# Linear attention on one core: stores cut into two halves of 64 partitions, and a longer TensorE warm-up

## The chip, the cores and the metric

The kernel runs on one core of a Trainium2 chip. Its engines work side by side: TensorE multiplies matrices (the profile lists its matmuls as PE and its weight loads as PEld), VectorE (DVE), ScalarE (ACT) and GpSimd (POOL) work on elements, and SyncE (SP) issues most of the transfers, which sixteen DMA engines carry out. Each engine runs its own instructions in order and waits for the others through semaphores. A transfer raises its semaphore by 16 when all of it has landed.

The metric is the time of one execution on the device, in microseconds (us).

## The reference

For each of 32 heads, with 2048 rows of 128 values in q, k and v (bfloat16):

```python
phi_q = jnp.where(q > 0, q + 1, jnp.exp(q)) + 1e-6
phi_k = jnp.where(k > 0, k + 1, jnp.exp(k)) + 1e-6
kv = jnp.einsum("bhsd,bhse->bhde", phi_k, v)
z = jnp.einsum("bhsd->bhd", phi_k)
num = jnp.einsum("bhqd,bhde->bhqe", phi_q, kv)
den = jnp.einsum("bhqd,bhd->bhq", phi_q, z)[..., None] + 1e-6
return num / den
```

So per head 1.5 MB is read, 0.5 MB is written, and between them stand two elementwise functions, a 128 x 128 product summed over all rows, a second product, and a division.

## The kernel before

**Tiling.** A head is laid out as 128 partitions with 16 rows each (`rows`, line 260): a partition holds 4,096 contiguous bytes of k, of q or of the output. One transfer moves a head of one tensor, 512 KB. Loads have six buffers for each tensor (`NBI`), stores ten (`NBO`), each with a semaphore of its own.

**One head.** ScalarE takes exp(k) (L328), VectorE caps it at 1 (L334), GpSimd makes the positive part of k (L330) and adds the two for five of the sixteen tiles (L339). TensorE sums phi_k^T v and z into `kvz_ps` (L355), and ScalarE and VectorE copy that to `kvs_sb` (L363, L365). TensorE transposes q through an identity into `x_ps` (L373), ScalarE takes its exp in two halves (L384), ScalarE and VectorE its positive part (L387, L390), VectorE caps (L393). TensorE multiplies with `kvs_sb` into five banks of `o_ps` (`num`, L411 and L417). VectorE adds the epsilon to the denominators (L456), takes reciprocals (L460) and divides into `o_sb` (L432, L438); in the last three heads ScalarE shares the division (L447). SP stores the head (L472).

**Order.** No engine's order follows from the loops. `Plan.add` is given an engine and a key, a number that counts in heads; each engine runs its operations by rising key (`Plan.order`, L54). `Plan.emit` works out which semaphores an operation must wait for from the tiles that it reads and writes, and leaves out a wait that an earlier one already covers. A writer of an output buffer waits for all stores that still read it. TensorE's middle part, twenty-four heads, is a hardware loop of four turns.

**Transfers.** All loads but the first v go through SP (L320), at about seven to eight heads ahead of their use by key. A store has the key `late = h + 1.0 + 0.18 * h`, so stores slip further behind the loads from head to head; after the last load the remaining stores follow. The last two heads go out in pieces of 6 and 10, and of 6, 6 and 4 tiles, so that the end of the kernel waits for a small one. When all is issued, SP waits for each store semaphore in turn (L152).

**Start.** While the first loads travel, TensorE runs nine matmuls of 128 x 512 on zeros (`warm`, L282 to L290, added at L296). They share one weight load; the second to ninth are emitted by the helper `mm_held` at L277.

Of the kernel before, what the change touches and what calls it, by code (L numbers as in the profile page):

```python
# [11 lines left out]
def _ap(base: bass.AP, elem_offset: int, dims):  # L12
    return bass.AP(base.tensor, base.offset + elem_offset, [list(base.ap[0])] + [list(d) for d in dims])
# [162 lines left out]
def bass_standalone__linear_attn_elu__prompt_kernel(  # L176
# [8 lines left out]
    NT = 16  # L185
# [3 lines left out]
    NBI = 6  # L189
    NBO = 10  # L190
# [20 lines left out]

    PIECES = {NH - 2: ((0, 6), (6, NT)), NH - 1: ((0, 6), (6, 12), (12, NT))}
    EXTRA = {NH - 2: 0, NH - 1: 1}
    LOOP, TURNS = 3, 4

    qf = q.rearrange("b h s d -> (b h) s d")
# [2 lines left out]
    of = out.rearrange("b h s d -> (b h) s d")  # L219

    with ExitStack() as es:
        def sb(name, shape, dt):
            return es.enter_context(nc.sbuf_tensor(name, shape, dt))
# [14 lines left out]
        o_sb = sb("o_sb", [P, NBO, NT, D], bf16)  # L238
# [11 lines left out]
        def dma_sem(name):  # L250
            return dsems[name]

        for n, c in (("k", NBI), ("q", NBI), ("v", NBI), ("o", NBO + 3), ("x", 1)):
            for i in range(c):
                dsems[(n, i)] = es.enter_context(nc.semaphore(f"s_{n}{i}"))

        block = es.enter_context(nc.Block())
        pl = Plan()

        def rows(x, h):  # L260
            return x[h].rearrange("(p j) d -> p (j d)", j=NT)
# [7 lines left out]
               reads=[("id0",)], writes=[("ident",)])  # L269
# [5 lines left out]
        def mm_held(pe, out, lhsT, rhs, start, stop):  # L275

            return pe.add_instruction(mybir.InstMatmult(  # L277
                name=nc.get_next_instruction_name(), engine=mybir.EngineType.PE, ldweights=False,
                ins=[pe.lower_ap(rhs), pe.lower_ap(lhsT)], outs=[pe.lower_ap(out)], start_tensor_calc=start,
                stop_tensor_calc=stop, tile_size=(P, P), tile_position=(0, 0), bass_skip_group_check=True))  # L280

        def warm(n):  # L282

            def f(pe):
                for w in range(n):
                    o = o_ps[:, (2 + w % 3) * 512:(3 + w % 3) * 512]
                    w_sb, zeros = warm_sb[:, :], _ap(warm_sb[:, :], 0, [[0, 4], [1, P]])
                    last = mm_held(pe, o, w_sb, zeros, True, True) if w else pe.matmul(o, lhsT=w_sb, rhs=zeros, start=True, stop=True)
                return last
            return f  # L290
# [2 lines left out]

        pl.add("act", -9, lambda a: a.activation(rden_sb[:, 0, 0:1], warm_sb[:, 0:1], ACT.Exp), reads=[("warm",)],
               writes=[("rden", 0, 0)])
        pl.add("pe", -9, warm(9), reads=[("warm",)], writes=[("banko", 2), ("banko", 3), ("banko", 4)])  # L296

# [6 lines left out]
        for h in range(NH):  # L306
# [3 lines left out]
            bi, b2, b3, bo = h % NBI, h % 2, h % 3, h % NBO  # L310

            def load(name, buf, src, key, h=h, bi=bi):
# [4 lines left out]
                if name == "v":  # L317
# [11 lines left out]
                   reads=[("k", bi)], writes=[("ek", b2)])  # L329
            pl.add("pool", h, lambda g, bi=bi, b3=b3: g.tensor_scalar(rk_sb[:, b3, :], k_sb[:, bi, :], BIG, 0.0,  # L330
                                                                      op0=ALU.min, op1=ALU.max),
                   reads=[("k", bi)] + ([("emq", 1)] if h == 2 else []), writes=[("rk", b3), ("rkx", b3), ("phik", b3)])
            pl.add("dve", at("emk", -3 + 0.95),
                   lambda d, b2=b2, b3=b3: d.tensor_scalar(emk_sb[:, b3, :], ek_sb[:, b2, :], 1.0, EPS, op0=ALU.min, op1=ALU.add),  # L334
                   reads=[("ek", b2)], writes=[("emk", b3)])

            def added(x, b3=b3):
# [3 lines left out]
                reads=[("emk", b3), ("rkx", b3)] + ([("emq", (h - 1) % 3)] if h else []), writes=[("phik", b3)])  # L341

            def kv(pe, tiles, srcs, h=h, bi=bi, b3=b3):
                for j in tiles:
# [16 lines left out]
                   reads=[("emk", b3), ("rk", b3), ("v", bi), ("ones",), ("vones",)], writes=[("bankkv",)])  # L361
            pl.add("pe", at("kv", -1.2), lambda pe, kv=kv: kv(pe, ADD, (rk_sb,)), reads=[("phik", b3), ("v", bi)], writes=[("bankkv",)])
            pl.add("act", at("kvs", -0.95), lambda a, b3=b3: a.activation(kvs_sb[:, b3, 1:], kvz_ps[:, 1:NC], ACT.Copy),  # L363
                   reads=[("bankkv",)], writes=[("kvs", b3)])
            pl.add("dve", at("zs", -1 + 0.905), lambda d, b3=b3: d.tensor_scalar(  # L365
                kvs_sb[:, b3, 0:1], kvz_ps[:, 0:1], kvz_ps[:, NC:NC + 1], None, op0=ALU.add),
                   reads=[("bankkv",)], writes=[("zs", b3)])
# [14 lines left out]
            for half in (0, 1):  # L382
                pl.add("act", h - 1.1 + 0.05 * half,
                       lambda a, b2=b2, c=cols(half): a.activation(eq_sb[:, b2, c], xT_ps[:, c], ACT.Exp),  # L384
                       reads=[("bankx", half)], writes=[("eq", b2, half)])
            pl.add("act", h - 1.0,
                   lambda a, b3=b3, c=cols(1): a.activation(rq_sb[:, b3, c], xT_ps[:, c], ACT.Relu),  # L387
                   reads=[("bankx", 1)], writes=[("rq", b3, 1)])
            pl.add("dve", at("rq", -2 + 0.948),
                   lambda d, b3=b3, c=cols(0): d.tensor_scalar(rq_sb[:, b3, c], xT_ps[:, c], 0.0, None, op0=ALU.max),  # L390
                   reads=[("bankx", 0)], writes=[("rq", b3, 0)])
            pl.add("dve", at("emq", -2 + 0.955),
                   lambda d, b2=b2, b3=b3: d.tensor_scalar(emq_sb[:, b3, :], eq_sb[:, b2, :], 1.0, EPS, op0=ALU.min, op1=ALU.add),  # L393
                   reads=[("eq", b2, 0), ("eq", b2, 1)], writes=[("emq", b3)])
# [4 lines left out]
            def nbank(b, h=h):  # L399
                return ("bankx", b) if h == NH - 1 and b < 2 else ("banko", b)  # L400
# [20 lines left out]
            for bank in range(NB):  # L421
                pl.add("pe", h + 0.7 + 0.001 * bank, num(bank), reads=phi,
                       writes=[nbank(bank)] + ([nbank(0)] if bank == 1 else []))
# [28 lines left out]
            for g, (b0, b1, place_d, runs) in enumerate(groups):  # L452
# [6 lines left out]
                    reads=banks, writes=[("den", b3, g)])  # L459
                pl.add("dve", key + 0.01, lambda d, b3=b3, b0=b0, b1=b1: d.reciprocal(  # L460
                    rden_sb[:, b3, 4 * b0:4 * b1], den_sb[:, b3, 4 * b0:4 * b1]),
                    reads=[("den", b3, g)], writes=[("rden", b3, g)])
                if g == 0:
                    pl.add("dve", h + 0.911, last_tile, reads=[nbank(0), nbank(1), ("rden", b3, 0)], writes=[("o", bo, NT - 1)])
                for n, (eng, t0, t1, *place_a) in enumerate(runs):
                    pl.add(eng, h + place_a[0] if eng == "act" else key + 0.012 + 0.004 * n,
                           div_act(t0, t1) if eng == "act" else div(t0, t1),
                           reads=[nbank(b) for b in range(t0 // 3, (t1 + 2) // 3)] + [("rden", b3, g)],
                           writes=[("o", bo, t) for t in range(t0, t1)])

            def store(t0, t1, key, slot, h=h, bo=bo):
                pl.add("sp", key, lambda sp: sp.dma_start(rows(of, h)[:, t0 * D:t1 * D],  # L472
                                                          o_sb[:, bo, t0:t1].rearrange("p j d -> p (j d)")),
                       reads=[("o", bo, t) for t in range(t0, t1)], dma=("o", slot))

            late = h + 1.0 + 0.18 * h
            for n, (t0, t1) in enumerate(PIECES.get(h, ((0, NT),))):
                store(t0, t1, late + 0.01 * n, bo if n == 0 else NBO + EXTRA[h] + n - 1)

# [29 lines left out]
```

## Time and profile before

| what | value |
|---|---|
| time, median of three runs | 170.68 us (170.63 to 170.9) |
| profiled execution: time, and span from first to last instruction | 170.68 us, 168.8 us |
| granted TensorE clock, mean over the span | 0.994 |
| busy: PE, PEld, DVE, ACT, POOL | 158.0, 151.7, 149.6, 157.3, 105.5 us |
| moved by DMA | 67.31 MB, 399 GB/s on average |
| in the hardware queue that SP feeds | 22688 packets, 98.5% of 16 engines' span |
| stores of a whole head | 30 of 512 KB, 13.8 us from issue to landing at the median |
| SP waiting at the end for stores to land | 3.3 us |

The span is counted from the first to the last instruction; what lies around it makes up the rest of an execution's time. Busy times of TensorE are modelled, since matmuls are pipelined. A DMA's time to landing counts from its issue, so it holds the time in the queue. "DMA share" is the mean busy share of the sixteen DMA engines, and can pass 1 by a little because records of packets overlap.

### The profile page before, as it was taken

To read this page: it belongs to the slowest core of one execution; us is meant where nothing else is said; L and a number is where in the kernel's file an instruction comes from. 1 tells how busy PE (TensorE), PEld (TensorE's weight loads), DVE (VectorE), ACT (ScalarE), POOL (GpSimd) and SP (SyncE) were. 2 spreads that over 40 slices of the span, in tenths; PEclk is the share of its full clock that TensorE was granted. 3 is DMA by queue.
4 is the path that set the end of the run, shared out by engine and by line. 5 is a ranking of instruction groups with operands and counts; after the bars stand their busy time and mean duration, and the time that the engine had idled before them with its cause. 6 is when DMAs were issued, how large, how long until landed. Compare 5 with 4: busy or idle time off the path is not lost.

```text
span 168.8 us, 6570 instructions
## 1 busy us (share of the span) xinstructions
PE 158.0 (94%) x3089; PEld 151.7 (90%) x2401; DVE 149.6 (89%) x293; ACT 157.3 (93%) x180; POOL 105.5 (62%) x72
## 2 busy tenths in 40 slices
PE   7588999999999999999999999999999999999940
PEld 0488999999999999999999999999999999999830
DVE  0144999999999999999999999999999999999870
ACT  4599999999999999999999999999999999996960
POOL 3836866666677776666667776666667776666000
PEclk9999999999999999999999999999999999999997
DMA  5999999999999999999999999999999999999982
GB/s 204 412 414 411 412 406 409 406 415 408 411 414 409 415 416 415 418 413 419 415 414 415 416 413 420 413 419 415 413 416 418 417 414 415 411 413 415 412 333 104
DMA packets 22848, 67.31 MB, mean 399 GB/s; under 512 B 2097, under 2 KB 2609, under 8 KB 22833
## 3 DMA queue, kind: packets, MB, share of 16 engines
q1 hardware_dynamic: 22688, 66.59, 98.5%
q10 hardware_dynamic: 144, 0.52, 0.8%
q8 instruction: 9, 0.15, 0.3%
q14 instruction: 7, 0.05, 0.1%
HBM read 50.33 MB, written 16.78 MB: 398 GB/s over the span
## 4 chain that ended last, share of the span: by engine, by line
PE 87%; DMA 3%; DVE 3%; ACT 3%; issue 0%; SPq 0%
PE kvz_ps L355 36%; PE o_ps L411 32%; PE x_ps L373 16%; DMA q_sb<-in_q_dram 3%; DVE o_sb L438 1%; PE o_ps L277 1%; ACT eq_sb L384 1%; PE o_ps L417 1%; PE kvz_ps L277 1%; ACT ek_sb L328 1%; ACT rq_sb L387 1%; DVE emk_sb L334 0%; DVE rden_sb L460 0%; DVE den_sb L456 0%; SPq L320 0%
## 5 line engine op out<-in xcount | busy, mean ns | idle before, releaser
L384 ACT ACTIVATE eq_sb<-x_ps 128x1024 bf16<-128x1024 bf16 x64 | 72.4, 1349 | 3.4 <-PE x_ps L373 3.4
L339 POOL TENSOR_TENSOR rk_sb<-rk_sb,emk_sb 128x640 bf16<-128x640 bf16 x32 | 44.7, 1396 | 47.4 <-DVE emq_sb L393 41.2
L328 ACT ACTIVATE ek_sb<-k_sb 128x2048 bf16<-128x2048 bf16 x32 | 72.2, 2256 | 1.7 <-DMA k_sb<-in_k_dram 1.7
L438 DVE TENSOR_TENSOR o_sb<-o_ps,rden_sb 128x768 bf16<-128x768 f32 (+2 forms) x63 | 68.0, 1119 | 0.1
L355 PE MATMUL kvz_ps<-v_sb,rk_sb 128*128 128x128 bf16 (+1 forms) x512 | 67.6, 218 | 0.0
L330 POOL TENSOR_SCALAR rk_sb<-k_sb 128x2048 bf16<-128x2048 bf16 x32 | 60.6, 1892 | 2.7 <-DMA k_sb<-in_k_dram 2.0
L411 PE MATMUL o_ps<-kvs_sb,emq_sb 128*128 128x129 bf16 x474 | 60.6, 220 | 0.3 <-DVE o_sb L438 0.3
L411 PE MATMUL o_ps<-kvs_sb,rq_sb 128*128 128x129 bf16 x474 | 60.6, 220 | 0.0
L355 PE MATMUL kvz_ps<-v_sb,emk_sb 128*128 128x128 bf16 (+1 forms) x352 | 55.4, 219 | 1.2 <-DVE kvs_sb L365 1.2
L277 PE MATMUL kvz_ps<-ones_sb,rk_sb 128*128 128x1 bf16 x388 | 53.3, 166 | 0.0
L355 PEld LDWEIGHTS kvz_ps<-v_sb,rk_sb 128*128 128x128 bf16 x512 | 47.0, 97 | 1.5
L411 PEld LDWEIGHTS o_ps<-kvs_sb,rq_sb 128*128 128x128 bf16 x474 | 46.2, 97 | 0.0
L411 PEld LDWEIGHTS o_ps<-kvs_sb,emq_sb 128*128 128x128 bf16 x474 | 45.4, 97 | 0.6 <-DVE o_sb L438 0.4
L387 ACT ACTIVATE rq_sb<-x_ps 128x1024 bf16<-128x1024 bf16 x32 | 43.7, 1366 | 0.0
L277 PE MATMUL kvz_ps<-ones_sb,emk_sb 128*128 128x1 bf16 x228 | 37.8, 167 | 0.0
L373 PE MATMUL x_ps<-ident,q_sb 128*128 128x128 bf16 x512 | 34.6, 222 | 1.7 <-DMA q_sb<-in_q_dram 1.7
L373 PEld LDWEIGHTS x_ps<-ident,q_sb 128*128 128x128 bf16 x512 | 30.6, 99 | 5.6 <-DMA q_sb<-in_q_dram 5.6
L355 PEld LDWEIGHTS kvz_ps<-v_sb,emk_sb 128*128 128x128 bf16 x352 | 33.9, 97 | 1.5 <-issue 1.5
L334 DVE TENSOR_SCALAR emk_sb<-ek_sb 128x2048 bf16<-128x2048 bf16 x32 | 21.8, 682 | 8.8 <-ACT ek_sb L328 8.8
L390 DVE TENSOR_SCALAR rq_sb<-x_ps 128x1024 bf16<-128x1024 bf16 x32 | 21.8, 680 | 2.5 <-ACT eq_sb L384 2.5
L393 DVE TENSOR_SCALAR emq_sb<-eq_sb 128x2048 bf16<-128x2048 bf16 x32 | 22.1, 691 | 0.4 <-ACT eq_sb L384 0.4
L363 ACT ACTIVATE kvs_sb<-kvz_ps 128x128 bf16<-128x128 f32 x32 | 20.3, 634 | 0.0
(39 smaller groups left out, 78.2 us busy)
## 6 DMA issues: line engine op xcount, KB each, us to landing
k_sb<-in_k_dram SPq DMA_DIRECT2D x32, 512.0 KB, 13.2
q_sb<-in_q_dram SPq DMA_DIRECT2D x32, 512.0 KB, 13.2
v_sb<-in_v_dram SPq DMA_DIRECT2D x31, 512.0 KB, 13.6
out_dram<-o_sb SPq DMA_DIRECT2D x30, 512.0 KB, 13.8
out_dram<-o_sb SPq DMA_DIRECT2D x3, 192.0 KB, 4.7
v_sb<-in_v_dram ACTq DMA_DIRECT2D x1, 512.0 KB, 4.4
out_dram<-o_sb SPq DMA_DIRECT2D x1, 320.0 KB, 5.6
out_dram<-o_sb SPq DMA_DIRECT2D x1, 128.0 KB, 4.0
```

The lines of the kernel that those rows point to most:

```text
L277: return pe.add_instruction(mybir.InstMatmult(name=nc.get_next_instruction_name(), engine=mybir.EngineType.PE, ldweights=False, ins=[pe.lo ...
L328: lambda a, bi=bi, b2=b2: a.activation(ek_sb[:, b2, :], k_sb[:, bi, :], ACT.Exp),
L330: pl.add("pool", h, lambda g, bi=bi, b3=b3: g.tensor_scalar(rk_sb[:, b3, :], k_sb[:, bi, :], BIG, 0.0, op0=ALU.min, op1=ALU.max), reads=[( ...
L334: lambda d, b2=b2, b3=b3: d.tensor_scalar(emk_sb[:, b3, :], ek_sb[:, b2, :], 1.0, EPS, op0=ALU.min, op1=ALU.add),
L339: pl.add("pool", h + 0.5, lambda g, added=added: g.tensor_tensor(out=added(rk_sb), in0=added(rk_sb), in1=added(emk_sb), op=ALU.add), reads ...
L355: last = pe.matmul(kvz_ps[:, 1 - l:NC + r], lhsT=w, rhs=rhs, start=first, stop=fin, skip_group_check=True)
L373: last = pe.transpose(xT_ps[:, j * P:(j + 1) * P], q_sb[:, bi, j * P:(j + 1) * P], ident[:])
L384: lambda a, b2=b2, c=cols(half): a.activation(eq_sb[:, b2, c], xT_ps[:, c], ACT.Exp),
L387: lambda a, b3=b3, c=cols(1): a.activation(rq_sb[:, b3, c], xT_ps[:, c], ACT.Relu),
L393: lambda d, b2=b2, b3=b3: d.tensor_scalar(emq_sb[:, b3, :], eq_sb[:, b2, :], 1.0, EPS, op0=ALU.min, op1=ALU.add),
L411: last = pe.matmul(o_ap, lhsT=x[:, b3, t * P:(t + 1) * P], rhs=kvs_sb[:, b3, :], start=first, stop=not first)
L438: return lambda d: d.tensor_tensor(out=o_sb[:, bo, t0:t1, :].rearrange("p (a b) d -> p a b d", b=n), in0=_ap(nfull(b), 512 * b + NC * (t0 ...
```

## The change

Two constants and one branch change. Each of the stores of heads 0 to 29 is issued as two transfers, the first for partitions 0 to 63 and the second for partitions 64 to 127, each 256 KB and with a semaphore of its own (thirteen output semaphores become twenty-three). Both wait for the whole head, as the single store did, and stand next to each other in SP's order. The stores of the last two heads stay as they are. The warm-up before the first head has twelve matmuls instead of nine.

```diff
     EXTRA = {NH - 2: 0, NH - 1: 1}
+    PARTS = ((64, 64),)
     LOOP, TURNS = 3, 4
...
-        for n, c in (("k", NBI), ("q", NBI), ("v", NBI), ("o", NBO + 3), ("x", 1)):
+        for n, c in (("k", NBI), ("q", NBI), ("v", NBI), ("o", 2 * NBO + 3), ("x", 1)):
...
-        pl.add("pe", -9, warm(9), reads=[("warm",)], writes=[("banko", 2), ("banko", 3), ("banko", 4)])
+        pl.add("pe", -9, warm(12), reads=[("warm",)], writes=[("banko", 2), ("banko", 3), ("banko", 4)])
...
             late = h + 1.0 + 0.18 * h
+
+            if h not in PIECES and len(PARTS[h % len(PARTS)]) > 1:
+                r0 = 0
+                for n, r in enumerate(PARTS[h % len(PARTS)]):
+                    pl.add("sp", late + 0.01 * n, lambda sp, h=h, bo=bo, r0=r0, r=r: sp.dma_start(
+                        rows(of, h)[r0:r0 + r, :], o_sb[r0:r0 + r, bo].rearrange("p j d -> p (j d)")),
+                        reads=[("o", bo, t) for t in range(NT)], dma=("o", bo if n == 0 else NBO + 3 + bo))
+                    r0 += r
+                continue
             for n, (t0, t1) in enumerate(PIECES.get(h, ((0, NT),))):
```

## The prediction

> **What bounds the kernel now.** I read the page's span and busy shares first, then the slices and queues, the chain that ended last, the table by stretches, and last the waits of the store queue.
>
> ```profile
> span 168.8 us, 6570 instructions
> PE 158.0 (94%) x3089; PEld 151.7 (90%) x2401; DVE 149.6 (89%) x293; ACT 157.3 (93%) x180; POOL 105.5 (62%) x72
> ...
> DMA  5999999999999999999999999999999999999982
> ...
> q1 hardware_dynamic: 22688, 66.59, 98.5%
> ...
> PE 87%; DMA 3%; DVE 3%; ACT 3%; issue 0%; SPq 0%
> ...
> out_dram<-o_sb SPq DMA_DIRECT2D x30, 512.0 KB, 13.8
> ```
>
> Two resources are full from start to end. TensorE holds 87% of the chain, and the 16 DMA engines show 9 in every slice but the outer ones. A store lands 13.8 us after its issue, so some eleven transfers are always queued. In the table by stretches the last column is what the DMA engines moved and the one before it their busy share:
>
> ```profile
> 16.00:155.00 139.00, 138.99 (x2818) 137.53 (x2204) 136.84 (x264) 137.86 (x147) 95.72 (x60) 1.00 1.03 414
> ...
> 162.00:164.00 2.00, 0.50 (x9) 0.33 (x6) 1.70 (x4) 1.68 (x6) 0.00 (x0) 1.00 0.86 337
> 164.00:166.00 2.00, 0.00 (x0) 0.00 (x0) 0.00 (x0) 0.00 (x0) 0.00 (x0) 1.00 0.68 253
> 166.00:168.80 2.80, 0.00 (x0) 0.00 (x0) 0.00 (x0) 0.00 (x0) 0.00 (x0) 0.66 0.06 24
> ```
>
> TensorE and DMA run level for 139 us, and after 164 only the transfers go on. A 0.06 share in the last stretch is one engine of sixteen. Each transfer raises its semaphore 16 times, once per DMA engine; in the trace those of the first load come within 0.24 us of each other, those of the last store 2.23 us apart (166.12 to 168.34). So the end is set by one late DMA engine, about 2.2 us behind the first, which had no pause: its packets follow each other to 167.9.
>
> The pace is the same in both directions. All 12,160 packets of 4,096 bytes, loads and stores, take 159 ns at the median (159 to 161 from the 5th to the 95th percentile), and one engine's share of a 512 KB transfer (eight such packets) lands 1.24 us after the one before it.
>
> **The change, part by part.** It is summed against the profiled execution's 170.68 us: 168.8 of span and 1.88 around it. The median of the three runs is the same 170.68.
>
> *More packets.* A half transfer has 64 rows of 4,096 bytes, four to an engine where eight were. Bytes and row packets stay; each engine gets one more semaphore packet per store, and the 4-byte packets took 9 ns each: 30 x 9 ns = 0.27 us, on the engine that ends last, hence at the end. Bound below: 0.
>
> *More issues on SP.* Thirty more DMA instructions at 0.33 us (the fastest store issue; the median, 1.26, is mostly a full queue pushing back) are 10 us of SP time over the run. They pass in time in which eleven transfers are queued anyway: nothing. Without that cover every load behind a store would go out 0.33 us later. Both halves stand next to each other in SP's order, so no load goes between them.
>
> *More waits.* The divisions that reuse one of the ten output buffers (heads 10 to 31) wait for two semaphores where they waited for one: 22 x 21 ns (a wait on VectorE's sequencer) = 0.46 us, at most. VectorE is busy 136.8 of 139 us, but TensorE sets the pace and the wait is issued beside the running instruction; I take 0. SP's ten more waits at the end (28 ns each) pass while the last store is in flight: 0.
>
> *What a transfer of 64 partitions takes.* The trace has none: every data transfer covers 128. Bound from below: half a transfer takes half the 1.24 us, so a store stays at 1.24. From above: a half takes what a whole takes, and a store 2.48, that is 1.24 more. [...] The nearest row is that equal pace: reads of HBM and writes of HBM cost the same to 1%, which speaks for a limit on the side that both share, the engine or SBUF. Between these two I lean to SBUF. [...]
>
> [...]
>
> *Warm-up of 12.* The nine end at 5.01; from 1.39 eight of them take 3.62 us, less the 0.6 of one's own length, so about 0.4 apart, and three more end near 6.3. The queries come at 6.71, so TensorE is free for them: cost 0. If q came 0.4 us earlier they would delay it by that. They may gain at the head:
>
> ```profile
> 1.18 5.48 DMA q_sb<-in_q_dram
> 6.71 1.05 PE x_ps L373 x8
> 7.78 1.94 ACT eq_sb L384 x2
> ...
> 17.43 0.89 PE x_ps L373 x16
> ```
>
> Eight transposes take 1.05 us here and sixteen take 0.89 later; the matmuls get short at about 9.8 us, where the trace's record of the full clock begins. With the clock up at 6.71 the eight would take 0.45: 0.6 less on the chain that starts ScalarE's run. In the sum it is 0, since TensorE's lead is lost behind the late DMA engines. [...]
>
> Sum: 170.68 + 30 + 0.27 - 2.2 = 198.7.
>
> **The rivals.** [...]
>
> *The change of size does nothing.* [...] Then the sum is 170.68 + 0.27, and a third of a microsecond to one and a half more where the extra instructions bring one more instruction load (1.3 us) onto the latest engine: 170.4 to 172.5.
>
> *Faster.* The halves cost nothing and the clock is up at 6.71; the first exponential starts 0.6 us sooner, TensorE and the last divisions with it. It decides only if no DMA engine is late by more than the last store's own flight, that is if the late engine has less than 2.2 us of backlog at 164: then the end comes up to 0.6 sooner, 170.1.
>
> **How the numbers follow.** A difference under 0.2% (0.34 us) can't be told from none with this kernel. Pairs that meet throughout: 0.37, 198.7, own range 188 to 206 (0.6 to 1.24 us a store, and the late engine). Pairs that part midway: 0.20. Nothing from the halves: 0.43, of which 0.19 ends faster by the warm-up, 0.09 within 0.2%, 0.15 slower by packets and instruction loads. So faster 0.19, same 0.09, slower 0.72. The range leaves out most of the faster cases and little else: 170.2 to 206.
>
> **What would show it.** Right: packets of 4,096 bytes near 300 ns among the stores, GB/s under 370 in the middle slices, the DMA's part of the chain above 20%, TensorE waiting for loads, idle shares on all engines. Wrong: 414 GB/s as before and 159 ns throughout, then the halves cost only their packets. The warm-up is right if the first eight transposes take 0.45 us. [...]

## The result and the profile after

The changed kernel takes 171.46 us at the median (171.26 to 171.51, six runs) against 170.63 (170.54 to 170.9, six runs) in the same comparison: a ratio of 1.0043, 95% interval 1.0033 to 1.0054. It is slower by 0.83 us, where the prediction had 198.7. The sign was right; the size was wrong by a factor of more than thirty. Executions more than 1.5% above the fastest of the same kernel are left out of the times below.

Of the page of the kernel after, the span, the count of DMA packets with the queue that SP feeds, and the group of half stores among the DMA issues:

```profile
span 169.6 us, 6608 instructions
...
DMA packets 23328, 67.33 MB, mean 397 GB/s; under 512 B 2576, under 2 KB 3088, under 8 KB 23312
...
q1 hardware_dynamic: 23168, 66.59, 98.7%
...
out_dram<-o_sb SPq DMA_DIRECT2D x60, 256.0 KB, 12.0
```

The reader sees 480 more packets in that queue than before: 30 more transfers with one semaphore packet on each of 16 engines, and not a byte more. Then the table by stretches, with the same columns as before (stretch, length, busy time of the five engines, granted clock, DMA share, GB/s):

```profile
12.00:16.00 4.00, 3.04 (x41) 2.87 (x25) 2.29 (x4) 4.00 (x5) 2.46 (x2) 0.59 1.03 411
16.00:155.00 139.00, 139.00 (x2820) 137.69 (x2205) 136.42 (x262) 138.18 (x147) 95.31 (x59) 1.00 1.03 414
162.00:164.00 2.00, 1.16 (x18) 0.98 (x18) 1.69 (x6) 1.33 (x6) 0.00 (x0) 1.00 0.96 336
```

The long middle is as it was, 414 GB/s with all engines full. The halves cost no bandwidth there: in the trace the first half store lands at 34.89 on the first engine and the second at 35.51, 0.62 us apart, and packets of 4,096 bytes still take 159 ns at the median (159 to 162 from the 5th to the 95th percentile). Two other things changed. Between 12 and 16 us the granted clock fell to 0.59 of full speed, and TensorE is still at work after 162 us for longer than before: its chain is late.

The trace's semaphore records split the 0.8 us by which the spans differ:

| | before | after |
|---|---|---|
| last store issued | 164.38 | 165.17 |
| its first of 16 landings | 166.12 | 166.87 |
| its last landing | 168.34 | 168.80 |
| span's end | 168.82 | 169.64 |

The last landing is 0.46 later, and from there to the end it takes 0.84 instead of 0.48, which is 0.36 more. TensorE's chain lost 0.65 to 0.8 us, but the last landing doesn't follow it one for one.

### The profile page after: what moved, and what is told of

Read it like the earlier page. It is cut to its first block, busy times and chain, and to the rows that moved or that the text cites. A ratio compares the mean times of both kernels' runs of the same rounds, so it can differ in the third digit from the quotient of the medians.

```text
span 169.6 us, 6608 instructions
## 1 busy us (share of the span) xinstructions
PE 159.0 (94%) x3092; PEld 151.5 (89%) x2401; DVE 150.3 (89%) x293; ACT 158.2 (93%) x180; POOL 105.6 (62%) x72
## 4 chain that ended last, share of the span: by engine, by line
PE 85%; ACT 5%; DMA 3%; DVE 3%; issue 1%; SPq 0%
PE kvz_ps L356 35%; PE o_ps L412 31%; PE x_ps L374 16%; DMA q_sb<-in_q_dram 3%; ACT eq_sb L385 2%; DVE o_sb L439 1%; PE o_ps L278 1%; ACT ek_sb L329 1%; PE o_ps L418 1%; PE kvz_ps L278 1%; ACT o_sb L448 1%; ACT rq_sb L388 1%; DVE emk_sb L335 0%; DVE rden_sb L461 0%; SPq L321 0%
## 5 line engine op out<-in xcount | busy, mean ns | idle before, releaser
L356 PE MATMUL kvz_ps<-v_sb,rk_sb 128*128 128x128 bf16 (+1 forms) x512 | 68.4, 219 | 0.0
L385 ACT ACTIVATE eq_sb<-x_ps 128x1024 bf16<-128x1024 bf16 x64 | 62.1, 1022 | 3.2 <-PE x_ps L374 3.1
L329 ACT ACTIVATE ek_sb<-k_sb 128x2048 bf16<-128x2048 bf16 x32 | 61.9, 1934 | 1.8 <-DMA k_sb<-in_k_dram 1.8
L374 PEld LDWEIGHTS x_ps<-ident,q_sb 128*128 128x128 bf16 x512 | 29.9, 98 | 5.6 <-DMA q_sb<-in_q_dram 5.6
L374 PE MATMUL x_ps<-ident,q_sb 128*128 128x128 bf16 x512 | 33.8, 219 | 0.5 <-DMA q_sb<-in_q_dram 0.5
L388 ACT ACTIVATE rq_sb<-x_ps 128x1024 bf16<-128x1024 bf16 x32 | 33.1, 1033 | 0.0
L394 DVE TENSOR_SCALAR emq_sb<-eq_sb 128x2048 bf16<-128x2048 bf16 x32 | 22.6, 707 | 0.4 <-ACT eq_sb L385 0.4
L433 DVE TENSOR_TENSOR o_sb<-o_ps,rden_sb 128x128 bf16<-128x128 f32 x31 | 9.0, 291 | 1.0
```

The costliest lines, as they stand in the source:

```text
L329: lambda a, bi=bi, b2=b2: a.activation(ek_sb[:, b2, :], k_sb[:, bi, :], ACT.Exp),
L356: last = pe.matmul(kvz_ps[:, 1 - l:NC + r], lhsT=w, rhs=rhs, start=first, stop=fin, skip_group_check=True)
L374: last = pe.transpose(xT_ps[:, j * P:(j + 1) * P], q_sb[:, bi, j * P:(j + 1) * P], ident[:])
```

## Experiments

**Which part costs: the halves or the warm-up?** Two candidates stood against each other: the clock that falls after a longer warm-up, and the DMA engine that lands last. First each part of the change alone. The halves without the longer warm-up:

```diff
-        pl.add("pe", -9, warm(12), reads=[("warm",)], ...
+        pl.add("pe", -9, warm(9), reads=[("warm",)], ...
```

> The stores in halves, the warm-up at nine as before. Theory A (the warm-up: twelve matmuls bring the clock up early, TensorE then waits 2.13 us for the second head's operands, the clock drops for 3.41 us and the whole chain runs 0.65 to 0.82 us later): no difference, 170.5 to 170.8. Theory B (the late DMA engine: every half adds a semaphore packet of about 15 ns to each engine, 30 of them to the one that lands last, and the kernel's own end grows by 0.3): the last landing 0.46 later, 171.3 to 171.5.

Measured: 171.66 against 170.69, ratio 1.0061 (1.0044 to 1.0077), above the range of theory B. The profiled execution is the fastest of the six (171.19), and what lies around the span makes 1.8 to 2.5 us of their times; their spans are 169.4 to 169.7, where the median of before is 168.8. So by its spans this kernel is as slow as the changed one, though in the profile TensorE's chain is not late at all: its last products start at 161.21, before at 161.30. And the kernel before with twelve warm-up matmuls, stores whole:

```diff
-        pl.add("pe", -9, warm(9), reads=[("warm",)], ...
+        pl.add("pe", -9, warm(12), reads=[("warm",)], ...
```

> Twelve warm-up matmuls, stores whole as before. Theory A: the slowdown comes back whole, 171.3 to 171.5, with a granted clock of 0.5 for 3.4 us between 12 and 16 us. Theory B: the same dip of the clock and a chain 0.65 to 0.82 us later, but the late DMA engine still has more than that queued at the end, so 170.6 to 170.8.

Measured: 170.77 against 170.69, ratio 1.0009 (1.0001 to 1.0018), less than a tenth of a per cent. Its stretch at the start, with the columns of the stretches above:

```profile
12.00:16.00 4.00, 3.05 (x41) 2.88 (x25) 2.28 (x4) 4.00 (x5) 2.47 (x2) 0.58 1.03 410
```

The dip of the clock is there, 0.58 in this stretch, and its last store is issued at 164.97 where before had 164.38. Still its last landing comes only 0.10 us later (168.44). So theory A falls: TensorE is late, and the end doesn't notice. The executions of before say the same: in these comparisons 24 of 64 have a mean granted clock of 0.976 to 0.980 and the others 0.985 to 0.996, and the median times of the two kinds are 170.71 and 170.72. What the dip does to TensorE is seen in the chains. Before, where the first transposes start at 6.71 and take 1.05, the chain's products at 16 us and at the end (start, length, what):

```profile
16.41 1.02 PE o_ps L411 x18
...
161.30 1.22 PE o_ps L411 x18
```

After, where the change moved all lines down by one:

```profile
6.64 0.64 PE x_ps L374 x8
...
17.23 1.02 PE o_ps L412 x18
...
161.95 1.22 PE o_ps L412 x18
```

In this profile with twelve matmuls the clock is up at 5.88 us instead of 9.85, and the eight transposes take 0.64 instead of 1.05. TensorE then does the first head's sums and the second head's transposes sooner, and waits 2.13 us for the second head's operands (1.20 before). The granted clock falls to 0.5 at 12.71 for 3.41 us, in which the matmul pairs of the second head's sums follow each other 0.14 us apart, where those of the first head took 0.08. The chain has gained 0.48 at ScalarE's first exponential (7.78 to 7.30) and is 0.82 late at 17 us.

That the three more matmuls made the clock rise sooner is not shown by one pair of profiles. In the traces of all fourteen kernels here, the four with twelve have it up between 3.73 and 5.88 us; of the ten with nine, four have it up between 4.43 and 5.26 and six between 9.85 and 12.71. Twelve make an early rise more frequent at most. Nor does the wait always cost the clock: in the run with two stores of 120 and 8 partitions (below), with nine matmuls, it is up at 5.26, TensorE waits 2.12 us at the same place, and it stays up.

**Does the late DMA engine set the end?** The kernel before, without the store of one middle head:

```diff
-            for n, (t0, t1) in enumerate(PIECES.get(h, ((0, NT),))):
+            for n, (t0, t1) in enumerate(() if h == 20 else PIECES.get(h, ((0, NT),))):
```

> The kernel before without the store of head 20 (that head's output is not written). If the late DMA engine sets the end, its queue is one store of 1.24 to 1.37 us shorter and the time falls by 1.0 to 1.4, to 169.2 to 169.6, until the last pieces are bound by the divisions. If TensorE's chain sets the end, 170.5 to 170.7.

Measured: 169.44 against 170.69, ratio 0.9932 (0.9917 to 0.9947): 1.25 us less, one store's share of a DMA engine. No store near the end was touched: before, this one's last landing was at 153.63, some 15 us ahead of the end, and taking it out moves the end by its whole length. The DMA queue sets it. The counterpart leaves the stores and mends TensorE's start:

```diff
-        pl.add("pe", -9, warm(9), reads=[("warm",)], ...
+        pl.add("pe", -9, warm(12), reads=[("warm",)], ...
+        pl.add("pe", -0.22, warm(9), reads=[("warm",)], writes=[("banko", 2), ("banko", 3), ("banko", 4)])
-        pl.emit(block, sems, dma_sem, ("pe", 1 + LOOP * 9, NBI * 9, TURNS))
+        pl.emit(block, sems, dma_sem, ("pe", 2 + LOOP * 9, NBI * 9, TURNS))
```

> Twelve warm-up matmuls, whole stores, and nine more matmuls on zeros between the second head's transposes and its first product, where TensorE waited 2.13 us. The clock stays up and the chain runs 0.4 to 0.6 us ahead of before from the second head on. If the late DMA engine sets the end, that is lost: 170.5 to 170.7. If TensorE's chain does, 170.0 to 170.3.

Measured: 170.81 against 170.69, ratio 1.0000 (0.9988 to 1.0011). The clock stays up in the same stretch:

```profile
12.00:16.00 4.00, 3.82 (x69) 2.86 (x44) 2.31 (x4) 4.00 (x6) 2.30 (x2) 1.00 1.04 414
```

and its chain runs 0.31 ahead of before, a little less than expected:

```profile
16.10 1.02 PE o_ps L412 x18
...
160.99 1.22 PE o_ps L412 x18
```

As a repair of the warm-up it is worth nothing here: the last landing is at 168.32, as before. That the added matmuls kept the clock fits this trace, but the kernel that kept it without them leaves the point open.

**What does a half transfer cost?** If each transfer has a fixed price on the late engine, quarters must cost three times the halves:

```diff
-    PARTS = ((64, 64),)
+    PARTS = ((32, 32, 32, 32),)
-        ... ("o", 2 * NBO + 3) ...
+        ... ("o", 4 * NBO + 3) ...
-                        ... dma=("o", bo if n == 0 else NBO + 3 + bo))
+                        ... dma=("o", bo if n == 0 else NBO * n + 3 + bo))
```

> Stores of heads 0 to 29 as four transfers of 32 partitions, warm-up of nine. If a transfer costs the late DMA engine a fixed amount (6 to 15 ns by the halves alone, where 30 more transfers moved the last landing by 0.18 to 0.46), 90 more give 0.5 to 1.4, and with the 0.3 of a longer end 171.5 to 172.4. If fewer partitions slowed the data itself (the prediction), quarter transfers would take far more than 0.31 us each and the time passes 195.

Measured: 172.88 against 170.74, ratio 1.0120 (1.0102 to 1.0138), above the range of the fixed price and nowhere near 195. Its last landing is at 170.33, 1.99 after that of before, and the last load, behind twenty stores, lands at 153.71 instead of 152.24, 1.47 later. Not all of that is the price of transfers. The late engine's landings at 145.24 and 147.32 are 2.08 apart, where the same step takes 1.23 before, and an instruction load of 8 KB travels at 146.0 which the kernel before hasn't got. That it met this engine is inferred from the times, since the trace doesn't name the engines. Without the 0.85 of this step, 90 more transfers cost 1.14, 13 ns each, and the 60 ahead of the last load 0.62, 10 ns each. For the halves, 0.46 / 30 gives 15 ns in the changed kernel and 0.18 / 30 gives 6 in the profiled run of the halves alone. So a transfer more costs the late engine some 6 to 15 ns, not far from the 9 ns of its semaphore packet.

**Where is the half rate, then?** The prediction had put the limit on the partitions' side of SBUF. The same cut was tried on loads of k:

```diff
-                pl.add("sp", key, lambda sp: sp.dma_start(dst, rws), writes=[(name, bi)], dma=(name, bi))
+                if name == "k":
+                    for n, r0 in enumerate((0, 64)):
+                        pl.add("sp", key + 0.001 * n, lambda sp, r0=r0: sp.dma_start(dst[r0:r0 + 64, :], rws[r0:r0 + 64, :]),
+                               writes=[(("k", "m")[n], bi)], dma=(("k", "m")[n], bi))
+                    return
```

(and both readers of k name the second half too).

> The stores whole, the loads of k in two halves of 64 partitions with a semaphore each, warm-up of nine. The prediction's limit on the partitions' side, tried in the other direction: if writing 64 partitions runs at 60% of the rate or at half of it, each k load takes 0.83 to 1.24 us more, 32 of them 27 to 40 us: 195 to 210. If the DMA engine sets the pace there too, only 32 more transfers at 6 to 15 ns on the late engine: 170.8 to 171.5.

Measured: 216.34 and 219.31 us against 170.74, above the range. Here the limit is, with more force than forecast. The profiled execution is the one of 219.31. The shares of the chain on its page:

```profile
DMA 60%; PE 18%; SPq 6%; ACT 5%; DVE 4%; issue 2%; POOL 1%
```

and the stretch from 40 to 150 us:

```profile
40.00:150.00 110.00, 86.41 (x1647) 80.54 (x1287) 80.42 (x154) 85.40 (x86) 56.49 (x36) 1.00 1.04 308
```

The DMA engines are as busy as ever (1.04) and move 308 GB/s where before moved 415; every compute engine idles; the chain runs through DMA. Each k load costs 45.6 / 32 to 48.6 / 32, that is 1.43 to 1.52 us more than whole, though its lower and upper half alternate. That is more than the 1.24 of the upper bound: v's packets of 2,048 bytes, which were not cut, take up to 164 ns (95th percentile) instead of 84, so the neighbours are slowed too. The control cuts the same loads by columns, so that each half still spans 128 partitions:

```diff
+                    for n, c0 in enumerate((0, HALF)):
+                        pl.add("sp", key + 0.001 * n, lambda sp, c0=c0: sp.dma_start(dst[:, c0:c0 + HALF], rws[:, c0:c0 + HALF]),
```

> The loads of k cut in two by columns, 128 partitions of 2,048 bytes each, a semaphore each; warm-up of nine, whole stores. A control for the k loads in halves of 64 partitions: if it was the number of transfers or the second semaphore that took 219 us, this is as slow. If it was the 64 partitions, it costs 32 more transfers at about 20 ns and 8 more packets each at about 5 ns on the late engine: 171.3 to 173.

Measured: 172.67 against 170.72, ratio 1.0108 (1.0093 to 1.0123). Neither the number of transfers nor the second semaphore made the 219 us; the 64 partitions did.

For stores two readings were left: that reading out of SBUF has no such limit, or that the two alternating halves dodge it. A store that reads the lower half twice can't dodge:

```diff
-                        rows(of, h)[r0:r0 + r, :], o_sb[r0:r0 + r, bo].rearrange("p j d -> p (j d)")),
+                        rows(of, h)[r0:r0 + r, :], o_sb[0:r, bo].rearrange("p j d -> p (j d)")),
```

> As the halves alone, but both transfers of a store read partitions 0 to 63 (the lower half of each head's output is written twice and the upper half never). [...] If reading 64 partitions is limited and the halves alone only escaped it by drifting apart, a store takes up to 1.24 us more: 180 to 208. If reads out of SBUF have no such limit, the same as the halves alone: 171.2 to 171.8.

Measured: 180.36 against 170.72, ratio 1.0567 (1.0543 to 1.0590), at the edge of the one range and far from the other. The stretches tell why:

```profile
40.00:150.00 110.00, 110.00 (x2234) 108.96 (x1747) 109.21 (x210) 110.00 (x118) 74.94 (x46) 1.00 1.03 415
...
154.00:172.00 18.00, 7.81 (x144) 7.13 (x118) 9.00 (x25) 7.89 (x22) 1.40 (x1) 0.78 0.89 203
```

Up to 150 us, with three loads between two stores, nothing is lost: 415 GB/s. After the last load, when stores follow stores, the rate is halved to 203 GB/s, and 82% of the 4,096-byte packets take 280 to 330 ns. Their median is 307 ns. So the limit shows in reading too, and with loads in between it doesn't. The last run asks whether that is all, with the full output and only another order: the lower halves of heads 22 to 27 in a row, then the upper ones.

```diff
-                    pl.add("sp", late + 0.01 * n, lambda sp, ...
+                    pl.add("sp", 32.87 + 0.01 * (h - 22) if n and 22 <= h <= 27 else late + 0.01 * n, lambda sp, ...
```

> As the halves alone, with another order at the end only: of heads 22 to 27 the six lower halves go out one after the other, then the six upper halves. The output is whole. If reading one half of the partitions is limited to half the rate whenever transfers of the same half follow each other with nothing else between, as the stretch after 150 us suggests for the lower half read twice, twelve half stores take up to 0.62 us more each: packets of about 304 ns there and 175 to 179. If that stretch was slow for another reason, the same as the halves alone: 171.1 to 171.8.

Measured: 174.75 against 170.74, ratio 1.0230 (1.0213 to 1.0247), just short of the range: 4.0 us more than before, of which the halves alone had made some 0.9.

```profile
158.00:163.00 5.00, 3.94 (x65) 3.31 (x58) 4.20 (x15) 4.38 (x15) 0.00 (x0) 1.00 0.80 218
```

In this stretch its packets of 4,096 bytes take 268 ns at the median, and 48% of them 280 to 330. In the changed kernel the same stores, alternating lower and upper, keep 95% of their packets under 165 ns between 152 and 158 us, at 410 to 420 GB/s. So the order decides: halves of one side in a row run at about half rate (203 and 218 GB/s in these stretches), halves between loads at the full one (415 up to 150 us in both runs).

Alternating halves keep it only for a time. Before and after, behind the last load:

```profile
155.00:160.00 5.00, 4.74 (x94) 4.37 (x70) 4.54 (x14) 4.66 (x12) 1.40 (x1) 1.00 1.02 410
160.00:162.00 2.00, 1.67 (x29) 1.55 (x28) 1.88 (x6) 1.54 (x7) 0.00 (x0) 1.00 0.93 376
...
155.00:160.00 5.00, 5.00 (x102) 4.80 (x79) 4.54 (x13) 4.01 (x10) 1.40 (x1) 1.00 1.02 388
160.00:162.00 2.00, 1.40 (x24) 1.10 (x20) 1.90 (x6) 2.00 (x7) 0.00 (x0) 1.00 1.01 348
```

From 158 to 164 us a quarter of the changed kernel's packets take over 165 ns, where before it was 7%, some of them 280 to 330 as in the bunched stores. By then a half store's sixteen landings are up to 4.8 us apart, so the engines are at different stores; that this puts more of them in the same half at once is the author's guess. The late engine loses nothing there: between 155 and 166 us it takes 1.27 to 1.43 us for two halves, before 1.23 to 1.45 for a whole store. Why the limit doesn't show with loads in between (415 GB/s in the run with the lower half twice), no run tells. Why loads of alternating halves are slow at once (308 GB/s), and stores are not (414), stays open too.

**Can the late engine be spared?** A transfer of 120 rows can't be dealt evenly to sixteen engines:

```diff
-    PARTS = ((64, 64),)
+    PARTS = ((128,),) * 27 + ((120, 8),) * 2 + ((128,),)
```

> Whole stores but for heads 27 and 28, which go out as 120 and 8 partitions; warm-up of nine. 120 rows can't be dealt evenly to sixteen DMA engines but can to fifteen. If the late DMA engine is the sixteenth, it is spared two stores of 1.24 to 1.37 us and the end falls until the next engine or the divisions bound it, about 1 us: 169.3 to 169.9. If another engine is the late one, it gets the same or 0.15 us more per store: 170.7 to 171.3.

Measured: 171.29 against 170.74, ratio 1.0038 (1.0023 to 1.0053). In the trace the part of 120 lands on fifteen engines and the part of 8 on eight. The last landings of the two parts of head 27 are 163.52 and 163.71, 1.5 and 2.5 us behind the next to last: the late engine carries a share of both, so it isn't the one that was spared. With the repaired warm-up on top, that is the same sizes and the second warm-up call of the repair:

```diff
-    PARTS = ((64, 64),)
+    PARTS = ((128,),) * 27 + ((120, 8),) * 2 + ((128,),)
+        pl.add("pe", -0.22, warm(9), reads=[("warm",)], writes=[("banko", 2), ("banko", 3), ("banko", 4)])
-        pl.emit(block, sems, dma_sem, ("pe", 1 + LOOP * 9, NBI * 9, TURNS))
+        pl.emit(block, sems, dma_sem, ("pe", 2 + LOOP * 9, NBI * 9, TURNS))
```

> The same two stores as 120 and 8, with twelve warm-up matmuls and nine more in the second head's wait. If the late engine is the sixteenth and its queue no longer covers TensorE's chain, the 0.3 that the chain is ahead shows: 169.0 to 169.6, 0.2 to 0.4 under the kernel without the added matmuls. If the late engine is another, 170.5 to 171.1.

Measured: 171.29 against 170.74, ratio 1.0033 (1.0019 to 1.0047), above both ranges: no version here that stores the whole output beats the kernel before.

**The longer end.** Both halves on one semaphore:

```diff
-        ... ("o", 2 * NBO + 3) ...
+        ... ("o", NBO + 3) ...
-                        ... dma=("o", bo if n == 0 else NBO + 3 + bo))
+                        ... dma=("o", bo))
```

> As the halves alone, but both halves of a store raise the same semaphore, so there are thirteen output semaphores as before the change and not twenty-three, and ten waits less at the end. If the ten semaphores and their waits cost the 0.3 us between the last wait and SP's drain, 0.3 less than the halves alone: 171.1 to 171.3. If the transfers alone cost, the same as the halves alone: 171.4 to 171.7.

Measured: 171.14 against 170.72, ratio 1.0032 (1.0020 to 1.0043). The profile's SP lines of the kernel after, behind the last wait for a store (count, length in ns, first and last start):

```profile
L222 SPq COMPARE_BRANCH  x1: 38/38/38, 168.9 to 168.9; - x1
L222 SPq DRAIN  x1: 81/81/81, 169.3 to 169.3; - x1
```

and the same lines of the kernel with one semaphore:

```profile
L222 SPq COMPARE_BRANCH  x1: 38/38/38, 168.9 to 168.9; - x1
L222 SPq DRAIN  x1: 7/7/7, 169.1 to 169.1; - x1
```

The extra 0.3 between the branch and the drain is gone, and from the last landing to the end it takes 0.48 again. But it isn't the number of semaphores: the quarters have forty-three and no such gap either (0.14 us from branch to drain). All four profiled kernels with 60 half stores and twenty-three semaphores have it. What makes it is open.

## Why the prediction was wrong

*What bounds the kernel.* Right. The late DMA engine sets the end: a store less takes 1.25 us off, TensorE's chain 0.3 ahead or 0.6 late takes or gives 0.1 at most. The lines that carried it were the last stretches and the landings 2.23 us apart.

*What a transfer of 64 partitions takes.* This term failed: the sum has 30 us for the thirty stores and takes off 2.2. No run shows either term; the last landing moved by 0.46 in all. The lean to the partitions' side over the engine was right as far as loads and bunched stores go (1.43 to 1.52 us more per k load, packets of 307 ns at the median where the lower half follows itself). No run shows the 60% of the rate in the expectation for the k loads: by the 1.24 us of a whole load, these ran at 45 to 46%. The step that fell is that a half costs the same wherever it stands: here the two halves stood side by side between loads, and ran at 159 ns a packet and 414 GB/s. Neither row used in the prediction, 159 ns and 1.24 us, spoke of that.

*Pairs that meet or part.* No run shows two DMA engines that hold each other up or stop doing so; the chances of 0.37 and 0.20 rest on no measured row. The first half stores already run at full rate (their first landings 0.62 us apart), with thirteen of sixteen landings within 0.46 us of each other. Slow packets come at the end instead, behind 158 us, where the engines are furthest apart: a quarter of them take over 165 ns.

*More packets.* Right in place and sign, and near in size: 0.27 was forecast for 30 packets of 9 ns, and the last landing moved by 0.46 in the changed kernel and by 0.18 in the profiled run of the halves alone.

*More waits.* SP's end was put at 0 and the profile shows 0.36. It isn't the waits themselves, which pass while the last store is in flight, as forecast; what makes it is open.

*More issues on SP.* Nothing in the middle, as forecast (414 GB/s). The one more instruction load that the rival "the change of size does nothing" had reckoned with did come, ten of 16 KB where there were nine; it travels at 163.8 us, and the late engine's landings, 0.6 to 0.7 us apart there, show no step.

*Warm-up.* The clock did rise before the first transposes, and the time at the end is untouched, as the sum had it. The eight transposes took 0.64 where 0.45 was forecast. Twelve matmuls had the clock up early in all four traces, but nine had it in four of ten, so how much of that is their doing is open. What the prediction missed is that TensorE, with the clock up early, got ahead of its operands and waited 2.13 us, and that the granted clock was then at 0.5 for 3.41 us; the "faster" rival fell to the late engine in any case.

The rival that came true is "the change of size does nothing" with its 170.4 to 172.5, which had 0.43 in all and 0.15 for its slower side. That the time still lies in the range of 170.2 to 206 says nothing for the 198.7: the range was drawn wide enough to take this rival in. The sign came out right by the packets and SP's end, not by the term that the forecast rested on.

## What to carry to other kernels

Before pricing a slower transfer, ask what stands next to it in the queue: the stores here ran at 203 to 218 GB/s where like followed like, at 415 with loads in between, and for a time at 414 where lower and upper halves alternated. For loads the other half hid nothing. Cutting the loads of one tensor into 64 partitions was dear (216 to 219 us), cutting stores nearly free, and neither gained anything. When sixteen engines share a queue, find the one that lands last: its total set the end here (a store less, 15 us ahead of the end, took 1.25 us off), and every transfer more cost it some 6 to 15 ns. Before dividing a delay by a number of transfers, look whether it came in steps. After a longer warm-up, look at what TensorE does next: here it waited 2.13 us for its operands, and the clock was at 0.5 for 3.41 us. One profile doesn't tell when the clock rises: with the same nine matmuls it came between 4.43 and 12.71 us.

## What the runs showed of the hardware

- Loading k in two halves of 64 partitions in place of 128 costs a 512 KB load 1.43 to 1.52 us more; cut by columns, about 0.06.
- Stores that read one half of the partitions in a row run at 203 to 218 GB/s; alternating halves at 410 to 420 between 152 and 158 us, and at 348 from there to 162.
- In the kernel before, each instruction load of 16 KB puts one DMA engine about 1.3 us behind: by 54 us, after six of them, six of a transfer's sixteen landings come some 1.7 us or more after the first, and they don't catch up while the queue is full.
- On the latest engine each store from 93 us on takes about 0.13 us longer than on the others in the kernel before, loads don't; no run shows why.
- A wait of 2.13 us in TensorE's work was followed by 3.41 us at half clock in the two traces with twelve matmuls and nothing in the gap; a wait of 2.12 us in a third kernel, with nine, was not. With nine matmuls on zeros in the gap the clock stayed up in both traces (1.00 between 12 and 16 us with whole stores).
